# V as the moving operand in three of the last head's four steps, the last piece of w2 split four ways, and the result in four transfers

## The chip, the cores and the metric

One core of one Trainium2 chip. The metric is the device time in microseconds (us), as the median of several executions. The profiled execution has a span a little under two microseconds shorter than its time (355.8 for 357.64). "Landing" is the moment at which one DMA engine's share of a transfer has arrived and been counted; the trace records each of them, but not which engine it was.

## The reference

A decode step for one token: a modulated layer norm, attention of 32 query heads over 8 cached key/value heads, an output projection, a second layer norm and a two-layer ReLU network.

```python
mod = (silu(c) @ w_mod) -> sa, ca, ga, sb, cb, gb
h = layernorm(x) * (1 + ca) + sa
x = x + ga * attention(h, k_cache, v_cache, wq, wo)   # 8 kv heads, 32768 keys, 128 wide
h = layernorm(x) * (1 + cb) + sb
x = x + gb * (relu(h @ w1) @ w2)                      # 512 -> 1792 -> 512
```

The caches are 128 MiB of bf16, the weights 14.5 MiB. Every byte is read once, so the time is that of a stream.

## The kernel before

All large loads go through one ring of four buffers of 32 KB per partition, in a fixed order, from one queue (SP). A load is issued when the last reader of the buffer that it overwrites has finished. The end of the order: `LAST` is the eighth head, its V comes in steps 0 and 1 (one buffer, 4 MB), 2, and 3 (2 MB each).

```python
stream += [("v", LAST, (0, 1)), ("v", LAST, (2,)), ("wo", 0), ("wo", 1), ("v", LAST, (3,)), ("wo", 2)]
stream += [("w1",)] + [("w2", i) for i in range(len(W2P))]
```

Counting four back in that list, V step 3 needs the buffer of V steps 0 and 1, wo's third piece that of step 2, w1 that of wo's first piece, and so on. The product of the weights P with V has two forms:

```python
def pv(g, u):
    ...
    if g == LAST:                      # V is stationary, 4 columns of P move: 64 matmuls a step
        if u == 0:
            o_tiles[g] = ps_o.tile([P, REP], F32, tag="oT", name="oT_ps", bufs=1)
        for j in range(TK):
            c0 = (16 * G + j % 16) * 32 + REP * (s0 + j // 16)
            nc.tensor.matmul(o_tiles[g][:], lhsT=Vsb[:, j, :], rhs=PT_g[:, c0:c0 + REP], ...)
        return
    ...
    for j in range(16):                # P is stationary, 512 columns of V move: 16 matmuls a step
        nc.tensor.matmul(o_tiles[g][:], lhsT=PT_g[:, c0:c0 + 16],
                         rhs=Vsb.rearrange("p (s j) d -> p s j d", j=16)[:, :, j, :], ...)
```

The second form needs a copy of its result out of PSUM and eight small products afterwards (four fp32 products in the code; the profile counts each fp32 product twice, so x8), to bring it into the transposed layout that the first form has at once. Before step 3 of the last head TensorE multiplies the first two pieces of wo (96 matmuls). The end of the kernel:

```python
    for part, (base, n) in enumerate(W2P):          # w2 in pieces of 1 MB, 512 KB, 256 KB
        w2_sb = need(("w2", part))
        ...
    nc.scalar.dma_start(out=out[0, 0].rearrange("(i n) -> i n", i=KT),
                        in_=o_bf[:].rearrange("(i r) n -> i r n", r=32)[:, 0, :])
```

## Time and profile before

| | us |
|---|---|
| time, median | 357.5 |
| V steps 0 and 1 of the last head begin / end | 327.24 / 330.81 |
| V step 3: load issued / landed / multiplied | 330.82 / 340.17 / 342.1 |
| last landing of w2 | 351.90 |
| last matmul ends | 352.35 |
| result landed | 354.76 |

Read it from the bottom: the last matmul follows the last landing by 0.45 us, and the stream that ends in this landing is full from early on until about 349 us. The lines that show this stand in the prediction. One more view of the same trace: stretches of two microseconds around the place where V step 3 queues. The first numbers are stretch and length, then the busy time of five engines, and the last three are TensorE's granted clock (1.00 is full, 0.50 half), the DMA engines' mean busy share, and GB/s.

```profile
330.00:332.00 2.00, 1.83 (x69) 1.77 (x67) 0.00 (x0) 0.00 (x0) 0.00 (x0) 0.50 1.05 426
332.00:334.00 2.00, 0.60 (x23) 0.60 (x23) 0.00 (x0) 0.00 (x0) 0.00 (x0) 0.50 0.99 385
334.00:336.00 2.00, 2.00 (x67) 2.00 (x65) 0.00 (x0) 0.00 (x0) 0.00 (x0) 0.50 1.06 455
336.00:338.00 2.00, 1.40 (x42) 1.31 (x40) 0.00 (x0) 0.00 (x0) 0.00 (x0) 0.50 0.91 381
```

TensorE runs at half clock, is idle for a quarter of these 8 us, and the DMA engines are full. Shares somewhat over 1 occur in this view and are read as full here.

### The profile page before, as it was taken

How to read it: one execution, taken by the hardware profiler on the slowest of the kernel's cores; microseconds unless marked ns; L12 is line 12 of the kernel's file. 1: busy time of each engine (PE TensorE's matmuls, PEld its weight loads, DVE VectorE, ACT ScalarE, POOL GpSimd, SP SyncE). 2: the span in 40 equal slices, each digit the busy share in tenths (PEclk: the TensorE clock that was granted, in tenths of full speed). 3: DMA queues.
4: the chain of work that ended last, by engine and by line, in shares of the span. 5: the costliest groups of instructions: out<-in, count | busy, mean ns of one | idle time of the engine just before them, and what ended most of it. 6: DMA issues, size and time to landing. Idle time of an engine off the chain costs nothing.

```text
span 355.8 us, 4200 instructions
## 1 busy us (share of the span) xinstructions
PE 274.2 (77%) x1859; PEld 129.9 (37%) x1859; DVE 188.0 (53%) x210; ACT 30.8 (9%) x74; POOL 8.5 (2%) x14
## 2 busy tenths in 40 slices
PE   0552875998689885998499849987799859987754
PEld 0540322343333342443244324433243324335753
DVE  8414696783297409661759157642937184832020
ACT  1022002201200120001100120012000110003000
POOL 9000000000000000000000000000000000000000
PEclk9999968799969996999699978998599969997555
DMA  8999999999999999999999999999999999999993
GB/s 321 442 422 440 431 427 442 429 425 438 435 426 438 431 422 446 427 431 440 424 442 435 422 443 427 431 437 427 431 437 428 427 438 433 424 437 424 408 411 130
DMA packets 6604, 149.69 MB, mean 421 GB/s; under 512 B 697, under 2 KB 698, under 8 KB 1594
## 3 DMA queue, kind: packets, MB, share of 16 engines
q1 hardware_dynamic: 6578, 149.43, 97.9%
q8 instruction: 14, 0.23, 0.2%
q14 instruction: 4, 0.03, 0.0%
q10 hardware_dynamic: 8, 0.00, 0.0%
HBM read 149.42 MB, written 0.00 MB: 420 GB/s over the span
## 4 chain that ended last, share of the span: by engine, by line
DMA 47%; PE 34%; DVE 14%; issue 3%; ACT 0%; SPq 0%; DVEq 0%
DMA Ksb<-in_A_k_cache_dram 42%; PE S_ps L343 18%; PE o_ps L412 12%; DVE KTt L334 11%; DMA Vsb<-in_A_v_cache_dram 3%; DMA w_sb<-in_B_w_dram 2%; PE oT_ps L402 1%; DVE PT_g L381 1%; PE oT_ps L429 1%; DVE S_g L349 1%; PE L_ps L386 0%; SPq L118 0%; PE attnT_ps L461 0%; PE mT_ps L359 0%; ACT X L426 0%
## 5 line engine op out<-in xcount | busy, mean ns | idle before, releaser
L343 PE MATMUL S_ps<-KTt,qbd 128*128 128x512 bf16 x512 | 134.5, 423 | 29.8 <-DVE KTt L334 29.7
L334 DVE STREAM_TRANSPOSE KTt<-Ksb 128x2048 f32<-128x2048 f32 x64 | 142.6, 2279 | 21.1 <-DMA Ksb<-in_A_k_cache_dram 17.0
L412 PE MATMUL o_ps<-Vsb,PT_g 128*16 128x512 bf16 x448 | 99.0, 379 | 0.0
L343 PEld LDWEIGHTS <-qbd 128*128 128x128 bf16 x512 | 53.8, 106 | 104.6 <-issue 53.8
L412 PEld LDWEIGHTS <-PT_g 128*16 128x16 bf16 x448 | 39.1, 90 | 56.8 <-issue 3.0
L436 DVE TENSOR_TENSOR oT_sb<-oT_ps,Linv 128x4 bf16<-128x4 f32 x8 | 1.3, 162 | 71.8 <-PE oT_ps L429 57.3
L349 DVE TENSOR_SCALAR_CACHE_REDUCE S_g<-S_ps 128x512 f32<-128x512 f32 x16 | 11.1, 691 | 41.3 <-PE S_ps L343 41.3
L314 ACT COPY qbd<-qrep_sb 32x128 bf16<-32x128 bf16 x32 | 9.4, 295 | 160.0 <-PE S_ps L343 158.9
L386 PE MATMUL L_ps<-Lexp,ones_f 128*128 128x4 f32 x16 | 3.9, 314 | 13.0 <-DVE Lexp L384 13.0
L426 ACT COPY X<-o_ps 16x512 f32<-16x512 f32 x7 | 4.0, 574 | 110.4 <-PE o_ps L412 110.4
L402 PE MATMUL oT_ps<-PT_g,Vsb 128*128 128x4 bf16 x256 | 7.3, 166 | 4.4 <-DMA Vsb<-in_A_v_cache_dram 2.8
L381 DVE STREAM_TRANSPOSE PT_g<-P_g 128x1024 bf16<-128x1024 bf16 x8 | 9.9, 1232 | 0.0
L429 PE MATMUL oT_ps<-osel,X 16*128 16x4 f32 x56 | 7.3, 250 | 2.5 <-ACT nbias L373 2.5
L197 PE MATMUL xc_ps<-one,c_bd 8*128 8x1 bf16 x4 | 0.3, 172 | 11.6 <-DVE c_bd L187 11.6
L376 ACT ACTIVATE P_g<-S_g,nbias 128x1024 bf16<-128x1024 f32 x8 | 9.2, 1147 | 0.2
L402 PEld LDWEIGHTS <-Vsb 128*128 128x128 bf16 x256 | 7.2, 105 | 4.5 <-DMA Vsb<-in_A_v_cache_dram 2.9
L359 PE MATMUL mT_ps<-ident_f,m_p 128*1 128x128 f32 x8 | 2.2, 269 | 8.4 <-DVE m_p L357 8.4
L386 PEld LDWEIGHTS L_ps<-Lexp,ones_f 128*128 128x128 f32 x16 | 3.6, 271 | 13.5 <-issue 13.4
L155 DVE COPY sel<-ident_bf 128x128 bf16<-128x128 bf16 x4 | 7.8, 3823 | 0.4 <-POOL ident_bf masks.py:199 0.4
L429 PEld LDWEIGHTS oT_ps<-osel,X 16*128 16x128 f32 x56 | 6.7, 186 | 3.1 <-ACT nbias L373 3.1
L292 PE MATMUL qT_ps<-hT,wq_sb 128*128 128x1 bf16 x128 | 3.6, 165 | 3.2 <-DMA wq_sb<-in_A_wq_dram 3.2
L359 PEld LDWEIGHTS mT_ps<-ident_f,m_p 128*1 128x1 f32 x8 | 0.6, 80 | 12.2 <-issue 9.2
(94 smaller groups left out, 79.4 us busy)
## 6 DMA issues: line engine op xcount, KB each, us to landing
Ksb<-in_A_k_cache_dram SPq DMA_DIRECT2D x16, 4096.0 KB, 29.7
Vsb<-in_A_v_cache_dram SPq DMA_DIRECT2D x15, 4096.0 KB, 25.5
wq_sb<-in_A_wq_dram SPq DMA_DIRECT2D x1, 4096.0 KB, 19.7
Vsb<-in_A_v_cache_dram SPq DMA_DIRECT2D x2, 2048.0 KB, 15.5
wm_sb<-in_w_mod_dram SPq DMA_DIRECT2D x1, 3072.0 KB, 10.2
wo_sb<-in_A_wo_dram SPq DMA_DIRECT2D x1, 2048.0 KB
wo_sb<-in_A_wo_dram SPq DMA_DIRECT2D x2, 1024.0 KB, 10.2
w_sb<-in_B_w_dram SPq DMA_DIRECT2D x1, 1792.0 KB, 10.5
```

Of the source, the lines that this page charges most:

```text
L155: nc.vector.tensor_copy(out=sel[:, hp, :].rearrange("p (a c) -> p a c", a=4), in_=src)
L314: nc.scalar.copy(out=o, in_=i)
L334: nc.vector.transpose(out=KTt[:].bitcast(F32), in_=Ksb[:, 32 * half:32 * half + 32, :].rearrange("p j d -> p (j d)").bitcast(F32),)
L343: nc.tensor.matmul(S_ps[:], lhsT=qbd[g % 2][:, hp, s, :], rhs=KTv[:, 16 * sl:16 * sl + 16, h, :, par], start=(t4 == 0 and sl == 0 and hp = ...
L349: nc.vector.tensor_scalar(out=S_tiles[g][:, G, :], in0=S_ps[:], scalar1=1.0, scalar2=None, op0=ALU.mult, op1=ALU.max, accum_out=m_tiles[g] ...
L376: nc.scalar.activation(out=P_g[:], in_=S_g[:].rearrange("p g f -> p (g f)"), func=ACT.Exp, bias=nbias[:], scale=scale, accum_out=l_g[:],)
L381: nc.vector.transpose(out=PT_g[:], in_=P_g[:])
L386: nc.tensor.matmul(L_ps[:], lhsT=ones_f[:], rhs=Lexp[:], start=True, stop=True)
L402: nc.tensor.matmul(o_tiles[g][:], lhsT=Vsb[:, j, :], rhs=PT_g[:, c0:c0 + REP], start=(u == 0 and j == 0), stop=(u == NTILE - 1 and j == TK ...
L412: nc.tensor.matmul(o_tiles[g][:], lhsT=PT_g[:, c0:c0 + 16], rhs=Vsb.rearrange("p (s j) d -> p s j d", j=16)[:, :, j, :], start=(u == 0 and ...
L426: nc.scalar.copy(out=X[:], in_=oT_ps[:])
L429: nc.tensor.matmul(oT_ps[:], lhsT=X[:, s * Dh:(s + 1) * Dh], rhs=osel[:, s, :], start=(s == 0), stop=(s == 3),)
```

## The change

Its intent, as far as the code tells: the last w2 piece should use only the DMA engines that are done early; V in steps 0 to 2 should use the form with a quarter of the instructions, with the copy and the small products done before step 3, so that only step 3 has to be short; and the result should be issued from two queues at once.

```diff
+        if key == ("w2", len(W2P) - 1):
+            for lo in range(0, P, 32):
+                stream_dma(
+                    t[lo:lo + 32].rearrange("p a b d -> p (a b d)"),
+                    src[lo:lo + 32].rearrange("(e q) a b d -> e q (a b d)", e=8),
+                )
+        else:
+            stream_dma(t[:], src)
 ...
-        if g == LAST:
+        if g == LAST and u == NTILE - 1:
 ...
             for j in range(TK):
-                    o_tiles[g][:], ..., start=(u == 0 and j == 0), stop=(u == NTILE - 1 and j == TK - 1),
+                    oT_tiles[g][:], ..., start=False, stop=(j == TK - 1),
             return
+        last = NTILE - 2 if g == LAST else NTILE - 1
 ...
+        if u == last:
+            X = spool.tile([16, 4 * Dh], F32, tag="X", name="X")
+            nc.scalar.copy(out=X[:], in_=o_tiles.pop(g)[:])
+            oT_tiles[g] = ps_o.tile([P, REP], F32, tag="oT", name="oT_ps", bufs=1)
+            for s in range(4):
+                nc.tensor.matmul(oT_tiles[g][:], lhsT=X[:, s * Dh:(s + 1) * Dh], rhs=osel[:, s, :],
+                                 start=(s == 0), stop=(g != LAST and s == 3))
 ...  (the same copy and products leave normalise())
-    nc.scalar.dma_start(out=..., in_=o_bf[:].rearrange("(i r) n -> i r n", r=32)[:, 0, :])
+    for i in range(KT):
+        eng = nc.scalar if i % 2 else nc.sync
+        eng.dma_start(out=out[0, :, i * P:(i + 1) * P], in_=o_bf[32 * i:32 * i + 1, :])
```

More of the change, by code (lines that the diff above doesn't have):

```diff
@@ L109, in load @@
             src = w2_v[:, a0:a0 + n]
-        stream_dma(t[:], src)
+        if key == ("w2", len(W2P) - 1):
[6 more added lines that the diff above has]
+            stream_dma(t[:], src)
         if kind in "kv":
@@ L318 @@
     PT_tiles, Linv_tiles = {}, {}
-    o_tiles = {}
+    o_tiles, oT_tiles = {}, {}
     def scores(g, u):
@@ L395, in pv @@
         G, s0 = u // 2, 4 * (u % 2)
-        if g == LAST:
-            if u == 0:
-                o_tiles[g] = ps_o.tile([P, REP], F32, tag="oT", name="oT_ps", bufs=1)
+        if g == LAST and u == NTILE - 1:
             for j in range(TK):
@@ L402, in pv @@
                 nc.tensor.matmul(
-                    o_tiles[g][:], lhsT=Vsb[:, j, :], rhs=PT_g[:, c0:c0 + REP],
-                    start=(u == 0 and j == 0), stop=(u == NTILE - 1 and j == TK - 1),
+                    oT_tiles[g][:], lhsT=Vsb[:, j, :], rhs=PT_g[:, c0:c0 + REP],
+                    start=False, stop=(j == TK - 1),
                 )
             return
+        last = NTILE - 2 if g == LAST else NTILE - 1
         if u == 0:
@@ L414, in pv @@
                 rhs=Vsb.rearrange("p (s j) d -> p s j d", j=16)[:, :, j, :],
-                start=(u == 0 and j == 0), stop=(u == NTILE - 1 and j == 15),
+                start=(u == 0 and j == 0), stop=(u == last and j == 15),
             )
+        if u == last:
[3 more added lines that the diff above has]
+            for s in range(4):
+                nc.tensor.matmul(
+                    oT_tiles[g][:], lhsT=X[:, s * Dh:(s + 1) * Dh], rhs=osel[:, s, :],
+                    start=(s == 0), stop=(g != LAST and s == 3),
+                )
     def part_of(g):
@@ L421, in normalise @@
     def normalise(g):
-        oT_ps = o_tiles.pop(g)
-        if g != LAST:
-            X = spool.tile([16, 4 * Dh], F32, tag="X", name="X")
-            nc.scalar.copy(out=X[:], in_=oT_ps[:])
-            oT_ps = ps_o.tile([P, REP], F32, tag="oT", name="oT_ps", bufs=1)
-            for s in range(4):
-                nc.tensor.matmul(
-                    oT_ps[:], lhsT=X[:, s * Dh:(s + 1) * Dh], rhs=osel[:, s, :], start=(s == 0), stop=(s == 3),
-                )
         i = part_of(g)
@@ L435, in normalise @@
         o_g = oT_sb[:, REP * g:REP * (g + 1)]
-        nc.vector.tensor_tensor(out=o_g, in0=oT_ps[:], in1=Linv_tiles.pop(g)[:], op=ALU.mult)
+        nc.vector.tensor_tensor(out=o_g, in0=oT_tiles.pop(g)[:], in1=Linv_tiles.pop(g)[:], op=ALU.mult)
         nc.vector.tensor_tensor(
@@ L533 @@
     nc.vector.tensor_tensor(out=o_bf[:], in0=o_rows[:], in1=x1_rows[:], op=ALU.add)
-    nc.scalar.dma_start(
-        out=out[0, 0].rearrange("(i n) -> i n", i=KT),
-        in_=o_bf[:].rearrange("(i r) n -> i r n", r=32)[:, 0, :],
-    )
+    for i in range(KT):
+        eng = nc.scalar if i % 2 else nc.sync
+        eng.dma_start(out=out[0, :, i * P:(i + 1) * P], in_=o_bf[32 * i:32 * i + 1, :])
 _INS = ['A_x', 'A_k_cache', 'A_v_cache', 'A_wq', 'A_wo', 'B_x', 'B_w1', 'B_w2', 'c', 'w_mod']
```

## The prediction

> **What bounds the kernel now.** I read the page's slices first, then the DMA table, then the chain of waits from 318 us on, then the timeline of the last 40 us, then stretches of 3.41 us for the granted clock.
>
> ```profile
> PEclk9999968799969996999699978998599969997555
> DMA  8999999999999999999999999999999999999993
> L412 PE MATMUL o_ps<-Vsb,PT_g 128*16 128x512 bf16 x448 | 99.0, 379 | 0.0
> L402 PE MATMUL oT_ps<-PT_g,Vsb 128*128 128x4 bf16 x256 | 7.3, 166 | 4.4 <-DMA Vsb<-in_A_v_cache_dram 2.8
> ```
>
> The DMA row is at 9 in all slices but the first and last: 149.69 MB at 421 GB/s make the time, and the engines matter only where they hold a transfer back. The clock row ends in three fives: the part the change touches runs on a half-speed TensorE. The two groups are the two ways of multiplying by V: L412 moves V (512 columns at a time, 16 matmuls a step), L402 holds V still (64 matmuls a step that move 4 columns).
>
> ```profile
> 327.38 3.42 PE oT_ps L402 x128
> 330.81 0.02 issue
> 330.82 9.35 DMA Vsb<-in_A_v_cache_dram
> 340.17 0.05 issue
> 340.22 1.88 PE oT_ps L402 x64
> ...
> 344.27 7.63 DMA w_sb<-in_B_w_dram
> 351.90 0.04 issue
> 351.94 0.41 PE ffn_ps L525 x7
> ```
>
> This is the chain of waits. The last head's V steps 0 and 1 share one ring buffer. Their 128 matmuls end at 330.81, and 0.01 us later the load of step 3 (2 MB) is issued: it had waited for that buffer. It lands at 340.17; then come step 3, wo, layer norm, w1, w2. The load is not late today: the trace's landing records put the last engine's part of the transfer ahead of it (wo's second piece) at 335.33, the first engine's at 332.10. So at 330.82 every engine still had 1.3 to 4.5 us of work. That is the slack which the change spends.
>
> ```profile
> 348.00:349.00 1.00, 0.59 (x22) 0.58 (x20) 0.00 (x0) 0.18 (x1) 0.00 (x0) 0.50 1.00 383
> 349.00:350.00 1.00, 0.43 (x20) 0.43 (x23) 0.00 (x0) 0.00 (x0) 0.00 (x0) 0.50 0.54 203
> 350.00:351.00 1.00, 0.74 (x32) 0.55 (x24) 0.00 (x0) 0.00 (x0) 0.00 (x0) 0.50 0.30 107
> ...
> 353.10 1.10 ACTq L534 DMA_DIRECT2D out_dram<-o_bf  x1
> ```
>
> The last two figures of a stretch are DMA share and GB/s. The stream ends raggedly: share 0.54, then 0.30. The last w2 piece has landings from 349.07 to 350.13 on eleven engines and from 350.94 to 351.90 on five. The single result transfer takes 1.10 us to issue; its data lands at 354.76 and the span ends at 355.77.
>
> **What the Trainium skill says.** (1) "TensorE: Matmul & The Clock Gate", Part 1: the clock is half until about one window of 3413 ns has been busy, and falls back after an idle one. The trace agrees: its clock stretches are multiples of 3.41 us, and after an earlier head's pause it needs a full window:
>
> ```profile
> 287.87:291.28 3.41, 1.21 (x3) 0.39 (x3) 3.41 (x2) 0.00 (x0) 0.00 (x0) 0.50 1.02 442
> 291.28:294.69 3.41, 3.41 (x9) 1.15 (x8) 3.41 (x3) 0.00 (x0) 0.00 (x0) 0.50 0.98 423
> 294.69:298.11 3.42, 3.42 (x17) 1.54 (x16) 1.90 (x1) 0.00 (x0) 0.00 (x0) 1.00 1.02 441
> 322.00:325.41 3.41, 2.59 (x16) 1.61 (x14) 0.39 (x3) 2.09 (x5) 0.00 (x0) 1.00 1.02 437
> 325.41:328.82 3.41, 2.00 (x62) 2.03 (x63) 1.45 (x3) 1.07 (x1) 0.00 (x0) 0.50 0.98 418
> 328.82:332.24 3.42, 3.01 (x114) 2.95 (x111) 0.00 (x0) 0.00 (x0) 0.00 (x0) 0.50 1.02 414
> ```
>
> (2) Same page, Back-to-back issue gap: N/1.2 ns cold, N/2.4 + 2.5 ns warm. Trace: starts of 512-column matmuls are 427 ns apart cold, 217 warm. (3) "DMA: Bandwidth & Descriptors", on why a DMA increments its semaphore by 16: the engine count is the largest number up to 16 that divides both slowest dimensions, on the lowest-numbered engines. 32 rows against 8 gives 8 engines. The trace does not name engines; but c_row (8 rows), queued behind the first weights, shows eight 128-byte packets following the weights' ends, and the three latest engines get none, so those lie in 8 to 15. (4) Same page, Issuing engines are not separate DMA queues: a second queue saves issue time only. No run shows that yet.
>
> **The change part by part.** *V moves again in steps 0 to 2.* Removed: 192 matmuls of 4 columns (3.42 us for 128, so 27 ns each). Added: 48 of 512 columns, one copy of the result (0.57 us on ACT, as for other heads) and 8 small products (1.05 us). Both forms can start at 327.24, when the softmax is ready and the clock has just fallen (325.41). If 512-column matmuls raise it as those of the earlier heads did, the first full window is 328.82 to 332.24. Until then 5.0 us at 427 ns make 11.7 matmuls; the other 20.3 of the first 32 cost 20.3 x 217 ns = 4.4 us. Steps 0 and 1 end at 336.65 instead of 330.81; step 2 ends at 336.65 + 16 x 0.217 = 340.1.
>
> So step 3's load is issued at 336.67, 5.85 us later. From issue to first packet the very first load took about 1.25 us (issued 0.74, packets from 1.76 to 2.23): data from 337.9. The engines ran dry between 332.1 and 335.3: the slowest loses 2.6 us, the fastest 5.8, and all restart level. Per engine there then follow, by packet durations of the trace: V 8 x 611 ns = 4.89, wo 8 x 309 = 2.47, w1 8 x 535 = 4.28, w2 32 x 84 = 2.69, then 1.34, and the last piece 0.67, or 1.34 on eight engines. Check on before: 335.33 + 16.34 = 351.67; measured 351.90. After: 337.9 + 17.0 + 0.2 = 355.1.
>
> TensorE's own chain: 340.1 + 1.7 (copy, small products) + 3.6 (96 projections at 37.5 ns, from 32 in 1.20) = 345.4; step 3 1.9 = 347.3; then as before from 342.1 to hidT's end at 348.8, 6.7: 354.0; 56 matmuls of w2 by 0.035 = 2.0: 356.0. The data chain gives 355.1 + 0.45 = 355.6. Before, the last matmul ended at 352.35. I take 355.8, **+3.4 us**. Skipped beside it: a stall of 1.56 us put down to issue at 333.40 in step 2, with an instruction fetch of 0.92 us started at 331.14; fewer instructions should spare it, but it held no transfer that was needed.
>
> *Last piece on engines 0 to 7.* On the ragged end of before, it would take the 16 KB off the late five if all lie in 8 to 15: end at 350.8 (the previous piece's last landing) instead of 351.9, with the previous 16 matmuls still to do, so about 0.5 us gained. After a level restart it costs up to 0.67 us; that is in the sum. Four issues at 0.36 us instead of one are hidden behind queued data.
>
> *Result rows.* One issue of 1.10 us becomes two on each of two queues. On SP a one-row load (x_row) took 0.23 us. If ACT's 1.10 comes from four strided rows, the end is 0.3 to 0.5 us earlier; if it is ACT's fixed cost per transfer, two cost 2.2, a loss. I take -0.1.
>
> Sum: 357.5 + 3.4 - 0.1 = **360.8 us**.
>
> **Rivals.** *The clock does not rise.* With 16 of 128 weight columns in use, L412 may not count as busy enough; stationary V in 328.82 to 332.24 was 3.01 of 3.42 us busy and did not raise it. Then 32 x 427 = 13.7 us, V issued at 340.9, w1 and the rest trickle out behind: about 368. Against it: the clock held through 318.58 to 322.00, all L412. I give it one in eight. *The transfer is hidden anyway*, because the load finds queued data or the clock stays up: even fully warm, 32 x 217 = 6.9 us put the issue at 334.2 and its data at 335.4, level with the slowest engine; then the ragged end and the result rows decide, 357 to 358. One in eight. *Fewer fetches and a level end win*: 356.5 to 357.5; little speaks for it, because the stream had no hole before.
>
> **Range and chances.** The free-running window moves the cold time between 3.4 and 6.8 us, the first 32 matmuls between 8.6 and 10.3, so 0.9 us each way; the order of copy and projections another 1; the hidden rival sets the low end. Range 358.3 to 363.8. Two per cent is 7.15 us, reached only by the cold rival: slower 0.10, same 0.89, faster 0.01.
>
> **What would show it.** Step 3's V load issued near 336.7 instead of 330.8; DMA share falling to near 0 somewhere in 333 to 338; the clock at 1.0 from about 332; V landing near 343; last w2 landing near 355. I am wrong if that load goes out before 334, if the DMA row has no hole, or if the clock stays at 0.5 (then far slower).

## The result

The changed kernel takes 362.02 us (361.87 to 362.82, 4 runs) beside 357.64 for the kernel before in the same rounds. The ratio is 1.0129, with a 95% interval of 1.0111 to 1.0146: slower by 1.3%, inside the predicted range and 1.2 us above the predicted 360.8. (A ratio is the mean time of one kernel's fast runs over that of the other's in the same rounds, so it is not quite the ratio of the medians.)

The page's slices after the change:

```profile
PEclk9999988999789987999799969997899969998955
DMA  8999999999999999999999999999999999999693
```

The DMA row now has a 6 in the slice from 333.2 us on, and the first of the last three fives in the clock row has become a 9: the clock is up where V moves, and the stream has a hole. The chain of waits, from the start of V to the last matmul (start, length, what):

```profile
327.16 11.81 PE o_ps L420 x48
338.97 0.02 issue
338.99 0.58 ACT X L427
339.58 0.04 issue
339.62 1.05 PE oT_ps L430 x8
340.67 3.30 PE attnT_ps L469 x96
343.97 1.72 PE oT_ps L409 x64
...
349.52 6.69 DMA w_sb<-in_B_w_dram
356.21 0.14 issue
356.34 0.41 PE ffn_ps L533 x7
```

Before, the same chain went through the 128 matmuls of L402 in 3.42 us and then through the load. Now 48 matmuls take 11.81 us, and the copy, the small products and the 96 projections stand one behind the other ahead of step 3. The chain shows only what the profile found to come last at each step; the hole is seen in the issues of the SP queue and in the stretches:

```profile
323.05 0.33 SPq L127 DMA_DIRECT2D wo_sb<-in_A_wo_dram  x1
335.53 0.33 SPq L127 DMA_DIRECT2D Vsb<-in_A_v_cache_dram  x1
338.99 0.33 SPq L127 DMA_DIRECT2D wo_sb<-in_A_wo_dram  x1
...
330.00:332.00 2.00, 2.00 (x11) 0.84 (x10) 0.00 (x0) 0.00 (x0) 0.00 (x0) 1.00 0.96 410
332.00:334.00 2.00, 2.00 (x11) 0.81 (x9) 0.00 (x0) 0.00 (x0) 0.00 (x0) 1.00 0.48 197
334.00:336.00 2.00, 2.00 (x11) 0.82 (x10) 0.00 (x0) 0.00 (x0) 0.00 (x0) 1.00 0.05 20
336.00:338.00 2.00, 2.00 (x11) 0.87 (x10) 0.00 (x0) 0.00 (x0) 0.00 (x0) 1.00 0.81 246
```

V step 3 is issued at 335.53 instead of 330.82. The DMA share falls to 0.48 and 0.05 where it was 0.99 and 1.06. Taking 1.00 as full, the four stretches lose 0.04 + 0.52 + 0.95 + 0.19 = 1.7 of a stretch of 2 us, or 3.4 us of all engines. The last w2 landing moves by 4.31 us, from 351.90 to 356.21, and the time by 4.4. What the hole leaves over is in slower packets: by the packet records, from 330 us to the last packet of w2 an engine was busy for 21.1 us of 25.6 on average, and before for 19.9 of 21.5. So some 3.0 us of the shift are idle engines and 1.2 us longer packets (V 5.36 us per engine for 5.10, w1 4.95 for 4.33, w2 5.10 for 4.75).

### The profile page after: what moved, and what is told of

Same layout as the page of the kernel before. It is cut to its first block, busy times and chain, and to the rows that moved or that the text cites. A ratio compares the mean times of both kernels' runs of the same rounds, so it can differ in the third digit from the quotient of the medians.

```text
span 360.2 us, 3937 instructions
## 1 busy us (share of the span) xinstructions
PE 280.1 (78%) x1723; PEld 129.0 (36%) x1723; DVE 188.0 (52%) x210; ACT 31.4 (9%) x75; POOL 8.5 (2%) x14
## 4 chain that ended last, share of the span: by engine, by line
DMA 52%; PE 25%; DVE 17%; issue 4%; SPq 1%; ACT 0%; DVEq 0%
DMA Ksb<-in_A_k_cache_dram 50%; DVE KTt L343 14%; PE S_ps L352 11%; PE o_ps L420 11%; DMA w_sb<-in_B_w_dram 2%; PE attnT_ps L469 1%; DVE PT_g L390 1%; PE oT_ps L430 1%; SPq L127 1%; DVE S_g L358 1%; PE oT_ps L409 0%; ACT X L427 0%; PE L_ps L395 0%; PE mT_ps L368 0%; DVE oA L445 0%
## 5 line engine op out<-in xcount | busy, mean ns | idle before, releaser
L420 PE MATMUL o_ps<-Vsb,PT_g 128*16 128x512 bf16 x496 | 110.9, 382 | 0.0
L420 PEld LDWEIGHTS <-PT_g 128*16 128x16 bf16 x496 | 43.7, 90 | 63.7 <-issue 4.9
L430 PE MATMUL oT_ps<-osel,X 16*128 16x4 f32 x64 | 8.4, 250 | 3.2 <-ACT nbias L382 2.1
L430 PEld LDWEIGHTS oT_ps<-osel,X 16*128 16x128 f32 x64 | 7.7, 186 | 4.3 <-ACT X L427 2.5
L469 PE MATMUL attnT_ps<-o_sb,wo_sb 128*128 128x1 bf16 x128 | 4.6, 172 | 0.3 <-DVE o_sb L461 0.3
L301 PEld LDWEIGHTS <-wq_sb 128*128 128x128 bf16 x128 | 3.5, 104 | 3.4 <-DMA wq_sb<-in_A_wq_dram 3.4
```

The source lines that it names most:

```text
L301: nc.tensor.matmul(qT_ps[:, hq:hq + 1], lhsT=wq_sb[:, kt, hq * Dh:(hq + 1) * Dh], rhs=hT[:, kt:kt + 1], start=(kt == 0), stop=(kt == KT - 1),)
L420: nc.tensor.matmul(o_tiles[g][:], lhsT=PT_g[:, c0:c0 + 16], rhs=Vsb.rearrange("p (s j) d -> p s j d", j=16)[:, :, j, :], start=(u == 0 and ...
L430: nc.tensor.matmul(oT_tiles[g][:], lhsT=X[:, s * Dh:(s + 1) * Dh], rhs=osel[:, s, :], start=(s == 0), stop=(g != LAST and s == 3),)
L469: nc.tensor.matmul(attnT_ps[:, ko:ko + 1], lhsT=wo_sb[:, r, :].rearrange("p (m ko) -> p ko m", ko=KT)[:, ko, :], rhs=o2_tiles[i][:, r:r + ...
```

## The experiments

Each was run beside the kernel before on the same chip. Unless said otherwise it was timed in five rounds (e_v_wos_b is a single profiled run). All results were correct.

| run | what it is | us | ratio to before (95%) |
|---|---|---|---|
| e_v | V part alone | 361.81 | 1.0129 (1.0114 to 1.0145) |
| e_w2 | w2 split alone | 358.13 | 1.0022 (1.0010 to 1.0034) |
| e_out | result rows alone | 357.13 | 0.9992 (0.9980 to 1.0004) |
| e_v_wos | e_v, load freed of the wait | 359.23 | 1.0062 (1.0037 to 1.0086) |
| e_v_warm2 | e_v, clock kept up | 360.46 | 1.0092 (1.0076 to 1.0109) |
| e_v_wos_warm | e_v, both | 357.68 | 1.0007 (0.9994 to 1.0020) |
| e_wos | before, load freed of the wait | 357.19 | 0.9995 (0.9983 to 1.0007) |
| e_s2 | V moves in step 2 alone | 360.20 | 1.0072 (1.0058 to 1.0086) |
| e_w2_k8 | w2 piece in 16 transfers of 8 rows | 361.25 | 1.0106 (1.0093 to 1.0119) |
| e_w2_k7 | w2 piece on 7 engines | 358.18 | 1.0024 (1.0010 to 1.0037) |
| e_w2_k7_out | e_w2_k7 and e_out | 358.24 | 1.0021 (1.0008 to 1.0033) |
| e_v_wos_b | second look at e_v_wos | 360.64 | one run |

### One part at a time

**e_v** is the middle part of the diff on the kernel before, with the w2 load and the result as they were.

> Only the V part of the change, put on the kernel before. Theory (the load of V step 3 waits for a buffer that the moving form of steps 0 and 1 frees 4.7 us later, and the DMA stream has a hole): this part is the whole loss, so 361.5 to 362.5 us, V step 3 issued near 335.5, DMA share near 0 around 335 to 336.5. Rival (the four issues of the last w2 piece or the result rows cost the time): within 0.5 us of the kernel before, 357.6.

Measured 361.81 us, the same ratio as the whole change. V step 3 was issued at 335.44, and the stretch from 334 to 336 had a DMA share of 0.03. The V part is the whole loss.

**e_w2** is the first part of the diff alone.

> Only the split of the last w2 piece, put on the kernel before. The trace of the changed kernel has sixteen landings for each of its four transfers, so I now think that they run on all sixteen engines. Theory (sixteen engines, so a split in name only): within 0.3 us of the kernel before, the end of the stream as ragged as before (first to last landing over 2 us). Rival (eight engines, as I predicted): 0.5 us faster, eight landings each.

Measured 358.13 us, 0.8 us slower than before: a little outside what I expected. What I expected of the form held: each of the four transfers has sixteen landings. The trace shows the instruction with 32 rows on the SBUF side; the eight-fold view on the DRAM side is contiguous, so that it can be read as 32 rows as well. The Trainium skill ("DMA: Bandwidth & Descriptors", on why a DMA increments its semaphore by 16) takes the dimensions "as the instruction carries it", and I had applied its rule to the view in the source. The split is one in name only, and its four transfers end at 352.29, 352.46, 352.62 and 352.78 where the one transfer ended at 351.90. Why the end is later was not settled: the piece before it, not split, also landed last at 352.13 instead of 350.80.

**e_out** is the last part of the diff alone.

> Only the four result rows on two queues, put on the kernel before. Theory (from the changed trace: from o_bf ready to the last landing 1.67 us, before 1.66): within 0.2 us of the kernel before. Rival (the shorter issue is worth it): 0.3 to 0.5 us faster.

Measured 357.13 us; the interval holds 1. In the changed kernel the issues look like this (SP and ACT, the timeline):

```profile
357.49 0.55 SPq L544 DMA_DIRECT2D out_dram<-o_bf  x2
357.50 0.84 ACTq L544 DMA_DIRECT2D out_dram<-o_bf  x2
```

Two issues on ACT end 0.84 us after the start and the last row lands at 359.16, 1.67 us after the first issue began. Before, one issue took 1.10 us and its data landed 1.66 us after it began. What is saved in issue time isn't saved at the end.

### The wait for the buffer

**e_v_wos** keeps V moving but takes away what makes step 3's load wait. The three pieces of wo share one buffer, so that V step 3 falls to the buffer that the seventh head frees:

```diff
-            t = ring.tile([P, WOP[key[1]][1] * REP, D], BF16, tag="slot", name="wo_sb")
+            if key[1] == 0:
+                loaded["wo_all"] = ring.tile([P, Hq, D], BF16, tag="slot", name="wo_sb")
+            g0, n = WOP[key[1]]
+            t = loaded["wo_all"][:, g0 * REP:(g0 + n) * REP, :]
```

> The V part as in e_v, but the three wo pieces share one ring buffer, so that V step 3 gets the buffer of the head before and waits for no step of the last head (issued near 323). Theory (two losses in a row: the hole in the stream, and TensorE's own chain that starts step 3 some 3.6 us later): the hole goes, DMA share stays over 0.9 until 348, but step 3 still starts near 344 and the end comes from TensorE's chain: 359 to 360.5 us. Rival A (the hole alone costs the time): 357 to 358. Rival B (the buffer has nothing to do with it): 361.5 to 362.5.

Measured 359.23 us, inside the main theory's range, but with a wide spread (see "The clock"). The load now goes out at 323.01 and the hole is gone:

```profile
323.01 0.33 SPq L121 DMA_DIRECT2D Vsb<-in_A_v_cache_dram  x1
...
332.00:334.00 2.00, 2.00 (x9) 0.77 (x8) 0.00 (x0) 0.00 (x0) 0.00 (x0) 0.87 1.07 455
334.00:336.00 2.00, 2.00 (x12) 0.81 (x9) 0.00 (x0) 0.00 (x0) 0.00 (x0) 1.00 0.98 422
336.00:338.00 2.00, 2.00 (x11) 0.87 (x10) 0.00 (x0) 0.00 (x0) 0.00 (x0) 1.00 1.02 426
```

One thing I had expected wrongly: the share didn't stay up until 348. The later two w2 pieces now wait for the shared wo buffer, and by the packet records only about half of the engines are busy from 347 to 348. It cost nothing, because the end comes from TensorE. Its chain has no wait for a DMA in it from V on:

```profile
345.27 1.73 PE oT_ps L403 x64
...
351.68 1.65 PE hidT_ps L515 x56
353.32 0.02 issue
353.35 0.19 ACT hidT L520
353.54 0.04 issue
353.58 1.69 PE ffn_ps L527 x56
```

So there are two losses, one behind the other: without the wait, TensorE's own work becomes the bound. It is 5.1 us late at the start of step 3 (345.27 here, 340.22 before). The profiled run took 360.58 us, more than the median, and its clock rose late, which is a part of that.

**e_wos** is the control: the same shared buffer on the kernel before.

> Control: the kernel before (V still in the last head) with the shared wo buffer alone. Theory (the load of V step 3 waited at no cost there, because the stream was full): within 0.5 us of the kernel before, and so 1.5 us or more under e_v_wos. Rival (the early load is a gain of its own, which hid part of the cost in e_v_wos): 1 us or more faster than before.

Measured 357.19 us, ratio 0.9995. Where V is stationary, the wait costs nothing that five rounds can see, and the early load gains nothing. In this kernel it doesn't matter when a load is issued, as long as that is before the queue runs dry.

### The clock

The runs of e_v_wos spread over 357.94 to 361.45 us, more than any other kernel's (next is e_s2, with 358.56 to 360.50). **e_v_wos_b** looks at the same kernel once more.

> A second look at the same kernel as e_v_wos, whose six runs spread from 357.94 to 361.45. Theory (the spread is the moment at which the clock rises in steps 0 to 2): the time goes with that moment; in the first look the clock rose at 332.52 and the run took 360.58; a rise near 329 should go with about 359, none of the two halves of a fall at all with about 357.7. Rival (the spread comes from the transfers): the same rise and another time, or the reverse.

It took 360.64 us with the clock rising at 332.72; the first look took 360.58 with the rise at 332.52. That agrees with the theory but tells nothing apart, because both looks fell in the same phase. The mean granted clock of each run was 0.897 in the three runs above 360 us and 0.900 to 0.910 in the four below, which fits, but is a mean over the whole run. **e_v_wos_warm** is the test that takes the cold time away: eight fp32 products (x16 in the profile) whose result is overwritten, in the pause between the softmax's first half and the start of V.

```diff
+        if g == LAST:
+            o_tiles[g] = ps_o.tile([16, 4 * Dh], F32, tag="o", name="o_ps")
+            for _ in range(8):
+                nc.tensor.matmul(o_tiles[g][0:1, 0:P], lhsT=nbias[:], rhs=ident_f[:], start=True, stop=True)
```

> e_v_wos with eight idle products (fp32, 128 columns, their result overwritten) in the pause of the last softmax, to keep TensorE's clock up. Theory (in e_v_wos TensorE's chain sets the end, and its cold time depends on where the clock's windows fall, hence the spread from 357.94 to 361.45): fewer cold matmuls in steps 0 to 2, so 357.5 to 359.0, with a smaller spread. Rival (the chain is not the bound, or such products do not count for the clock): 359.2 and the same spread.

Measured 357.68 us, spread 357.43 to 357.99. The timelines of TensorE, first e_v_wos and then e_v_wos_warm:

```profile
327.05 13.21 PE L414 MATMUL o_ps<-Vsb,PT_g 128*16 128x512 bf16 x48
```

```profile
325.04 1.91 PE L380 MATMUL o_ps<-ident_f,nbias 128*1 128x128 f32 x16
326.99 0.36 PE L395 MATMUL L_ps<-Lexp,ones_f 128*128 128x4 f32 x2
327.27 10.53 PE L420 MATMUL o_ps<-Vsb,PT_g 128*16 128x512 bf16 x48
```

The same 48 matmuls take 2.7 us less, and the profiled run 360.58 - 357.99 = 2.6 us less. The clock stayed at 1.00 from 292.72 to 340.51. The products touch no transfer, so the rival falls. That a run's time follows the moment of the rise was not seen directly, since no traced run of e_v_wos had an early rise. With both causes away, the V part costs nothing that five rounds can see (1.0007, interval 0.9994 to 1.0020).

**e_v_warm2** keeps the clock up but leaves the wait.

> e_v with the same eight idle products in the pause, but without the shared wo buffer: the clock alone is taken away as a cause, the buffer's dependence stays. In e_v_wos_warm steps 0 to 2 took 10.53 us instead of 13.16 with the clock at 1.0 throughout, so steps 0 and 1 end near 334.3. Theory (the load's wait makes a hole whose length is the end of steps 0 and 1 plus the 1.3 to 1.8 us to the first packet, less what is queued until 332.1 to 335.3): V step 3 issued near 334.3, a hole about 1.2 us shorter than in e_v, so 360.0 to 360.9 us. Rival in the prediction (with the clock up the transfer is hidden and the loss goes): 357 to 358. Rival (the clock has no part in it): 361.5 to 362.3.

Measured 360.46 us, inside the theory's range and well above the prediction's rival of a hidden transfer. V step 3 was issued at 333.74, first packets followed at 334.69, and the stretches show a shorter hole:

```profile
332.00:334.00 2.00, 2.00 (x11) 0.83 (x10) 0.00 (x0) 0.00 (x0) 0.00 (x0) 1.00 0.47 197
334.00:336.00 2.00, 2.00 (x11) 0.87 (x10) 0.00 (x0) 0.00 (x0) 0.00 (x0) 1.00 0.75 184
336.00:338.00 2.00, 1.33 (x8) 0.46 (x6) 0.00 (x0) 0.78 (x2) 0.00 (x0) 1.00 1.10 467
```

The rival had compared the load only with the slowest engine. The others had run dry between 332.12 and 335.03, and that time is lost too.

The four kernels make a table of two by two. Taking the wait away gains 2.6 us with the cold clock (361.81 to 359.23) and 2.8 us with the warm one (360.46 to 357.68). Keeping the clock up gains 1.4 us with the wait and 1.6 us without it. Together they make up the 4.4 us.

### Which step

**e_s2** moves V in step 2 alone; steps 0 and 1 are stationary as before.

> V moves in step 2 alone; steps 0 and 1 hold V still as before and free the shared buffer at their old time. Theory (the buffer of steps 0 and 1 is what costs): V step 3 issued near 330.5, no hole before 340, so most of the 4.4 us goes; TensorE's chain alone is some 2 us later at step 3, of which the wait for the last w2 piece hides all but about 0.5: 357.7 to 358.5 us. Rival (any 512-column form in the last head costs in proportion, 16 of 48 matmuls): about 358.9 with a hole a third as long.

Measured 360.20 us: both missed. V step 3 went out early enough at 331.15, as the theory said, and the hole of 334 to 336 was gone. But a new one had opened later:

```profile
331.15 0.33 SPq L118 DMA_DIRECT2D Vsb<-in_A_v_cache_dram  x1
337.22 0.33 SPq L118 DMA_DIRECT2D wo_sb<-in_A_wo_dram  x1
341.15 5.79 SPq L118 DMA_DIRECT2D w_sb<-in_B_w_dram  x4
...
336.00:338.00 2.00, 1.33 (x7) 0.45 (x5) 0.00 (x0) 0.75 (x2) 0.00 (x0) 0.95 0.92 393
338.00:340.00 2.00, 2.00 (x43) 1.98 (x44) 0.00 (x0) 1.10 (x1) 0.00 (x0) 0.90 0.84 291
340.00:342.00 2.00, 2.00 (x65) 2.00 (x64) 0.00 (x0) 0.00 (x0) 0.00 (x0) 0.50 0.71 291
```

Step 2 ran on the cold clock (6.08 us for 16 matmuls, from 331.12), so wo's third piece, which waits for step 2's buffer, went out at 337.22 instead of 334.23, and w1, which waits for the projections that follow, at 341.15 instead of 336.36. My theory had named one buffer; it is the ring. A step that frees its buffer late delays the load four places on, whichever that is. The clock has a part in this too: the two fastest of the six runs (358.56 and 359.91) have the highest mean clocks (0.899 and 0.905, the others 0.888 to 0.893). e_s2 with the clock kept up was not run.

### The last piece of w2

**e_w2_k8** puts the intent of the first part into a form that does use eight engines: transfers of eight rows, into a buffer of their own.

```diff
+            for lo in range(0, P, 8):
+                stream_dma(t[lo:lo + 8], src[lo:lo + 8])
```

> The kernel before with the last w2 piece really on eight engines: sixteen transfers of eight rows each, into a buffer of its own so that they are issued early. Theory (the late engines lie in 8 to 15, so the piece should be kept from them): eight landings per transfer, the stream's last landing near 350.8 instead of 351.9, 0.3 to 1.0 us faster than the kernel before. Rival (the late engines lie among 0 to 7, or sixteen small transfers cost what e_w2's four cost): 0.5 to 1.5 us slower.

Measured 361.25 us, 3.8 us slower, for a reason that neither theory had. The program has eight completion semaphores for its DMAs, and the trace shows each issue from the fifth on waiting for the earlier transfer of its semaphore: the sixth of the sixteen for w1's landing (346.79), the eighth for w2's second piece (351.25), and the last goes out at 353.94. It failed as a test of the time, but it has the landings (us, ordinary records of the trace):

```
w2's second piece, 16 landings: 347.92 ... 349.90 (ten), 350.38 350.39 350.45 350.47 350.58 351.24
first 8-row transfer, 8 landings: 348.10 348.15 348.36 348.46 349.13 349.40 349.64 350.10
```

The rows queued behind the second piece landed on all their eight engines before the six late engines had finished that piece. So the eight engines used do not include the late six. That part of the picture is right.

**e_w2_k7** uses it without running out of semaphores: one transfer of 119 rows (seven engines, 17 rows each) and one of 9.

```diff
+            stream_dma(t[0:119], src[0:119])
+            stream_dma(t[119:P], src[119:P])
```

> The intent of the change's first part, carried out in a form that the trace of e_w2_k8 supports: 119 rows of the last w2 piece in one transfer (119 = 7 x 17, so seven engines, 17 rows each) and 9 rows in a second, on the kernel before. In e_w2_k8 the eight-row transfers' eight landings lay at 348.1 to 350.1, with those of the piece before at 347.9 to 351.2, so the late six are not among the first eight. Theory (the late engines lie in 8 to 15 and are spared): seven and nine landings, the last piece landed by the time that the piece before has (350.8 to 351.3), 0.3 to 0.6 us faster than the kernel before. Rival (17 rows on one engine take longer than the late engines are late, or which engines are late differs from kernel to kernel): same or up to 0.7 us slower.

The landings were seven and nine, as planned. The time was 358.18 us, 0.8 us slower. In the profiled run (357.77 us, the fastest of the five) the seven engines ended at 351.47, but the late engines' share of the piece before ended at 351.68 instead of 350.80, so nothing was gained. Why the late engines are later when the last piece is not theirs stays open. **e_w2_k7_out** adds the result rows:

> e_w2_k7 with the four result rows on two queues, to see whether what is left of the change beats the kernel before. Theory (the two add): 0.5 to 0.9 us faster than the kernel before, about 356.7. Rival (neither is worth anything): 357.1 to 357.6.

Measured 358.24 us, slower than both the theory and the rival had it. No version that I tried beats the kernel before clearly; e_out and e_wos have intervals that hold 1.

## Why the prediction was right

**Buffer wait and hole (right).** The step "V step 3's load is issued when steps 0 and 1 end" is the whole case: e_v has the whole loss, e_v_wos without the wait is 2.6 us faster, and e_wos shows that the wait is free where the queue is full. The number is in part luck: the load went out 1.1 us sooner than predicted and the last piece was 0.6 us shorter, which hid more than half of what the stream took beyond its prediction. The 1.2 us by which 360.8 missed are what was left.

**When the load goes out (1.1 us too late).** Predicted 336.67, measured 335.53. The rise was right: as the Trainium skill has it ("TensorE: Matmul & The Clock Gate", Part 1), the clock rose after one busy window. It fell at 326.43, and the window that followed was busy for 3.24 of 3.41 us. In the prediction it fell at 325.41 and rose at 332.24, two windows later. The phase of the windows differs from run to run, and I had taken that of one trace. The other half of the rule, that the clock falls after an idle window, is not what the traces show, though the prediction said that they agree: its own line for 322.00 to 325.41 has TensorE busy for 2.59 of 3.41 us, and the clock fell. Nor is a busy window enough for the rise. The third line below, of the changed kernel, is a window filled with small matmuls, after which the clock fell; the fourth, of e_out, is one filled with 135 matmuls of V's stationary form, at the end of which it did not rise. So it is the form of the matmuls in steps 0 to 2 that raised it.

```profile
326.43:329.84 3.41, 3.24 (x9) 1.43 (x10) 0.20 (x2) 0.00 (x0) 0.00 (x0) 0.50 0.99 425
329.84:333.26 3.42, 3.42 (x17) 1.43 (x16) 0.00 (x0) 0.00 (x0) 0.00 (x0) 1.00 0.80 340
340.08:343.49 3.41, 3.41 (x92) 3.39 (x92) 0.00 (x0) 0.79 (x1) 0.00 (x0) 1.00 1.00 428
...
327.87:331.28 3.41, 3.41 (x135) 3.41 (x132) 0.00 (x0) 0.00 (x0) 0.00 (x0) 0.50 0.98 418
```

**From the restart to the last landing (too short: the mis-sized term).** Predicted 337.9 + 17.0 + 0.2 = 355.1, measured 356.21. First packets came from 336.50 on, 1.0 us after the issue, so the stream began sooner than predicted and still ended later. V's packets took 5.36 us per engine and not 4.89, w1's 4.95 and not 4.28. (In the kernel before, V took 5.10 and w1 4.33: the prediction had multiplied the typical packet, not the mean.) Of w1's 128 packets, 26 took over 560 ns, where before it was 2. All four kernels with a hole ahead of w1 have this (24 to 32 slow packets), and none of the others (0 to 2). I had used the packet durations of a stream without holes. That packets run into each other because a hole leaves all engines level would explain it, but I only argue that. Another explanation is as open: in these four kernels w1 was issued 1.0 to 1.5 us before its first packet, in the others 2.1 us or more. The engines also did not stay level, as the sum had it: they landed V within 342.26 to 342.64, but w1 within 349.43 to 351.20 and the last piece within 354.30 to 356.21, and the slowest of them set the end.

**Last piece on eight engines (wrong, small).** Predicted 1.34 us after a level restart; it ran on sixteen and landed 0.72 us after the piece before. It made the error above 0.6 us smaller than it would have been. One reading was off as well: before, the last piece has ten landings up to 350.13 and six from 350.94 on, not eleven and five; no term of the sum rests on that count.

**TensorE's chain (hidden, not the bound).** Predicted 356.0 beside a data chain of 355.6. Measured, step 3 ended at 345.69 instead of 347.3, for the most part because steps 0 to 2 ended 1.1 us earlier, and TensorE then waited for w1 and for all three w2 pieces: the data chain alone set the end. In e_v_wos the same chain is the bound, so its mechanism is real.

**Result rows.** Predicted -0.1; alone they measured -0.2 with an interval that holds zero.

**The rivals.** "The clock does not rise" fell: it rose on 512-column matmuls with 16 weight columns. "Hidden if the clock stays up" was not what happened here, and e_v_warm2 shows that it would not have held: 360.46 and not 357 to 358. "Fewer fetches and a level end" (356.5 to 357.5) fell with the result.

## What to carry to other kernels

In a kernel that one stream bounds, an engine's instruction is not paid for by its own time but by when it frees a buffer: count as many loads ahead as the ring has buffers and ask whether that load still goes out before the queue is dry. A faster-looking form of a product (fewer instructions, bigger tiles) that holds its input longer can lose there, and a clock that must warm up first makes it lose more. Check an intended engine count in the landings of the trace before counting on it.

## What the Trainium skill lacked or had wrong

- "TensorE: Matmul & The Clock Gate", Part 1, says that a busy window raises the clock and an idle one lowers it. It says little of what counts as busy, and the profile's busy time is not it. Here 135 matmuls that moved 4 columns each, busy 3.41 of 3.41 us (e_out), did not raise it; 512-column matmuls with only 16 weight columns, busy 3.24 of 3.41, did. And no idle window was needed for a fall: at the last head's pause the clock fell in all twelve traces without the extra products, after windows in which TensorE was busy for 1.19 to 2.68 us. In the two traces with eight fp32 products in that pause, busy 3.06 and 3.05 us, it stayed up (1.00 from 292.72 to 340.51 in e_v_wos_warm, from 295.53 to 339.91 in e_v_warm2).
- "DMA: Bandwidth & Descriptors", on how many engines a DMA uses: the rule held for 8 rows (8 landings), 119 rows (7) and 9 rows (9). It lacks that a contiguous view such as 8 x 4 x 1024 in the source does not give 8 engines: it ran on 16 (16 landings in e_w2).
- The same page calls two engines usually slower and ties it to GpSimd's transfers. Here, with transfers issued from SP, six of sixteen engines landed late at the end (350.94 to 351.90 beside 349.07 to 350.13), and e_w2_k8's landings show that these are not among the eight that an 8-row transfer uses.
- No page that I read has that packets are slower after a hole in the stream: w1's packet time per engine was 4.33 us without and 4.95 us with the hole, in the same program order. Why stays open.
